# Banded attention and a SoLU layer on one core: one fixed instruction order replaced by another

## The chip, the cores and the metric

The kernel runs on one core of a Trainium2 chip. The core has a matmul engine (TensorE, "PE" in the profile, with its weight loads as "PEld"), three engines for elementwise work (VectorE "DVE", ScalarE "ACT", GpSimd "POOL"), and a queue engine ("SP") that issues most DMA transfers. Each engine runs its own list of instructions strictly in order and waits for the others by semaphores. The metric is the device time of one execution in microseconds; less is better.

## The reference

Two layers in a row. The first is attention over 4 batches, 8 heads, 768 tokens and head size 64, where a query sees the 96 keys up to its own position and the first 8 keys of the sequence ("global" keys), with a bias that falls with distance:

```python
scores = scale * np.matmul(q, k.transpose(0, 1, 3, 2))
is_global = pos[None, :] < int(n_global)
is_local = (rel >= 0) & (rel < int(n_local))
dist = np.where(is_global & ~is_local, float(n_local), np.abs(rel))
scores = np.where(is_global | is_local, scores - slopes * dist, -1e9)
a = np.exp(scores - max); a = a / (sum(a) + 1e-09)
x = (a @ v) as 3072 tokens x 512
```

The second is a feed-forward layer on the 3072 tokens, 512 to 1024 and back to 512:

```python
h = x @ w_in
solu = h * softmax(h)
ln = (solu - mean(solu)) / np.sqrt(var(solu) + 1e-06) * g_ln
out = ln @ w_out
```

## The kernel before

**Attention.** Heads go in pairs, so a batch `b` has four pairs `p`. For each pair, keys and queries are loaded (`x32`, 384 KB each), cast to 16 bit (`cast_k`, `cast_q`, to `x16`), transposed on TensorE (L728) and copied from PSUM ("evacuated") to `kT` and `qT`. Batch 3 takes a DMA transpose (L762) in place of TensorE and evacuation. Values are loaded in two pieces per pair (L486) and cast into `v16`. The scores of a pair are made in two groups (64-key blocks with a window of 160 queries each, L874), ACT takes their exponential into `eb` (L882). In batch 0 the distance bias is added by matmuls (L860); in batches 1 to 3 the exponentials are multiplied by a factor `fb` (L890) instead. The global keys have scores of their own (L927, exponential L940). For each half of a batch (384 tokens, "unit" 0 and 1) TensorE sums the exponentials (L954, L963), ACT takes the logarithm (L970), DVE splits it (L979), TensorE spreads it over the rows (L1009), and ACT turns it into reciprocals `rr` (L1018). The attention products (L1053, L1043) come in two parts with a tiny DVE copy, `tick` (L1063), between them, and DVE multiplies them by `rr` into `xT` (L1078).

**Feed-forward.** For each of 24 tiles of 128 tokens: eight matmuls with `w_in` (L1112, "the projection"), exponential `ef` on ACT (L1118), `u` on DVE (L1121), its squares on ACT (L1128) or DVE (L1132), a transpose of `u` (on TensorE, L1147, for tiles 0 to 4, by DMA, L1137, for 5 to 23), and eight matmuls with the prepared `w_out` (L1193). A few POOL or DVE steps and two ACT steps for each group of three tiles give `rstd` (L1167 to L1176), which scales the result on ACT (L1204) or DVE (L1207), and it is stored (L1211). The last tile is done in two halves. `w_out` is prepared by eight products with `g` (`gw`, L633 to L639) and eight centring steps (L650).

**Casts and copies.** The helper `copy` has one line per engine: L266 for ACT, L268 for DVE, L270 for POOL. What a row of those lines is shows in its tiles: `x<-x` is a cast of keys or queries, `kT<-acc` and `qT<-acc` an evacuation, `v<-v` a cast of values, `w_in_sb<-late` a cast of a `w_in` half, `bw<-bw` and `fb<-fb` the copies of the bias and of the factor.

**The order.** A `Plan` collects all steps with what they read, what they may run on and which buffers they take. Nothing is scheduled at run time: four tables of numbers at the top of the file settle it. `ORDER` is the sequence in which the steps are issued, and with that the order of each engine and of SP's transfers. `SLOTS` gives the buffer of each step that takes one. `ENGS` gives the engine of each step that may run on several (casts, evacuations, factor products `fac`, `gw`, squares, `stats`, the scaling of the result). `WARM` puts filler matmuls (L1220, on a tile of ones) into TensorE's list, as "place in the order : PSUM bank : count":

```python
for s in plan.order():
    for spot, count in s["warm"]:
        for _ in range(count):
            nc.tensor.matmul(out=acc[:, spot, :], lhsT=busy16[:, 0:P], rhs=busy16, start=True, stop=True)
    if s["fn"] is not None:
        s["fn"]()
```

Of the kernel before, what the change touches and what calls it, by code (L numbers as in the profile page):

```python
# [29 lines left out]
FACT = {1, 2, 3}  # L30
SPLIT = False
ORDER = """
# [30 lines left out]
"""  # L63
SLOTS = """
# [10 lines left out]
"""  # L75
ENGS = """
# [4 lines left out]
"""  # L81
WARM = """
25:0:16 30:2:4 37:3:2 48:5:3 59:3:2 117:7:4 156:6:5
"""


# [1172 lines left out]
```

## Time and profile before

| what | value |
|---|---|
| median of 3 runs | 154.12 us (154.05 to 154.29) |
| span of the profiled execution | 154.3 us |
| instructions | 4774 |
| granted TensorE clock | full in all slices of the page |
| DMA, mean over the span | 236 GB/s, 36.35 MB |
| SP's transfers, share of 16 DMA engines | 95.0% |

The profiled execution's own time is its span, 154.3 us, 0.2 above the runs' median. Rows of a timeline are: start, duration, engine, line, operation, tiles written and read, shapes, count, and in brackets the idle time before and what ended it. Rows of equal kind that follow each other are merged, so a duration with "x4" is that of four. Rows by stage give for each stretch its length, the busy time of PE, PEld, DVE, ACT and POOL with the number of instructions, the granted clock, the DMA share and GB/s.

### The profile page before, as it was taken

The numbers are of one execution on the slowest core, as the hardware profiler recorded it, in microseconds if no ns is written. First come the engines' busy times: TensorE is split into PE (matmuls) and PEld (weight loads), VectorE is DVE, ScalarE is ACT, GpSimd is POOL, SyncE is SP. The second block draws the span as 40 slices with busy tenths as digits, with TensorE's granted clock in tenths as the row PEclk, the third lists the DMA queues.
The fourth block names the chain that finished last, engine by engine and source line by source line (L and its number), as shares of the span: only waits on it lengthen the run. The fifth ranks groups of instructions, "written<-read, shape, count | busy, mean of one in ns | idle before, by whom it ended". The sixth has DMA issues, their size and how long they took to land.

```text
span 154.3 us, 4774 instructions
## 1 busy us (share of the span) xinstructions
PE 144.9 (94%) x1877; PEld 77.9 (50%) x1877; DVE 119.2 (77%) x241; ACT 123.4 (80%) x212; POOL 60.0 (39%) x145
## 2 busy tenths in 40 slices
PE   6988899999899999799999999999999999999991
PEld 2545556477554565644544644544445644444451
DVE  6749988899999994789799959399893885799200
ACT  3959999799999888499999887878885676884642
POOL 7574456565394626852813115454212000110000
PEclk9999999999999999999999999999999999999999
DMA  4999999999996997999999999998999954488743
GB/s 146 373 305 337 307 391 327 347 340 398 295 264 108 242 285 175 220 270 233 262 196 154 271 141 244 171 233 161 189 231 259 247 141 97 90 222 223 224 166 136
DMA packets 76429, 36.35 MB, mean 236 GB/s; under 512 B 65456, under 2 KB 71928, under 8 KB 76408
## 3 DMA queue, kind: packets, MB, share of 16 engines
q1 hardware_dynamic: 76120, 35.54, 95.0%
q10 hardware_dynamic: 288, 0.52, 0.9%
q8 instruction: 14, 0.23, 0.7%
q14 instruction: 7, 0.06, 0.1%
HBM read 23.15 MB, written 6.29 MB: 191 GB/s over the span
## 4 chain that ended last, share of the span: by engine, by line
PE 44%; DMA 19%; ACT 9%; DVE 8%; POOL 7%; SPq 5%; issue 5%; POOLq 0%; DVEq 0%; ACTq 0%
PE acc L1193 16%; PE acc L1112 15%; DMA v<-in_v_dram 6%; DMA x<-in_q_dram 5%; DMA qT<-x 4%; PE acc L1053 3%; DMA kT<-x 3%; SPq L486 3%; ACT eb L882 2%; POOL x L270 2%; PE acc L728 2%; PE acc L874 2%; DVE uu L1121 2%; ACT ef L1118 2%; ACT rr L1018 1%
## 5 line engine op out<-in xcount | busy, mean ns | idle before, releaser
L1112 PE MATMUL acc<-w_in_sb,xT 128*128 128x512 f16 x192 | 44.4, 379 | 0.0
L1193 PE MATMUL acc<-gw_out_sb,late 128*128 128x512 f16 (+1 forms) x200 | 44.3, 371 | 0.1
L1121 DVE SCALAR_TENSOR_TENSOR uu<-ef,acc 128x1024 f16<-128x1024 f16 x24 | 29.2, 1216 | 5.4 <-ACT ef L1118 5.0
L882 ACT ACTIVATE eb<-acc 128x896 f16<-128x896 f32 (+1 forms) x32 | 29.3, 960 | 1.8 <-PE acc L874 1.8
L1193 PEld LDWEIGHTS <-late 128*128 128x128 f16 x200 | 18.9, 98 | 21.1 <-issue 0.9
L1118 ACT ACTIVATE ef<-acc 128x1024 f16<-128x1024 f32 x24 | 24.8, 1035 | 5.8 <-PE acc L1112 5.4
L1112 PEld LDWEIGHTS <-xT 128*128 128x128 f16 x192 | 18.1, 98 | 21.3 <-issue 1.1
L270 POOL CAST x<-x 128x768 f16<-128x768 f32 x17 | 14.4, 851 | 22.8 <-DMA x<-in_q_dram 7.8
L1078 DVE TENSOR_TENSOR xT<-acc,rr 128x384 f16<-128x384 f32 x32 | 16.3, 549 | 3.6 <-ACT rr L1018 1.9
L1053 PE MATMUL acc<-eb,v 64*64 64x160 f16 (+4 forms) x448 | 16.5, 221 | 2.1 <-DVE xT L1078 1.6
L1053 PEld LDWEIGHTS <-v 64*64 64x64 f16 x448 | 12.9, 106 | 6.6 <-issue 4.3
L1128 ACT ACTIVATE sqa<-uu 128x1024 f16<-128x1024 f16 x15 | 16.1, 1071 | 0.0
L1018 ACT ACTIVATE rr<-acc 128x768 f32<-128x768 f32 x16 | 12.7, 809 | 4.1 <-DVE tick L1063 2.5
L890 DVE TENSOR_TENSOR eb<-eb,fb 128x896 f16<-128x896 f16 (+1 forms) x19 | 14.1, 769 | 0.8 <-ACT eb L882 0.8
L270 POOL CAST v<-v 128x704 f16<-128x704 f32 (+3 forms) x13 | 8.8, 685 | 10.0 <-DMA v<-in_v_dram 9.3
L1220 PE MATMUL acc<-busy 128*128 128x512 f16 x36 | 10.8, 443 | 1.5 <-DVE busy L545 1.5
L728 PE MATMUL acc<-ident,x 128*128 128x128 f16 x144 | 11.1, 220 | 0.8 <-ACT x L266 0.7
L874 PE MATMUL acc<-qT,kT 64*64 64x160 f16 (+2 forms) x384 | 11.4, 227 | 0.3 <-ACT qT L266 0.3
L1132 DVE SCALAR_TENSOR_TENSOR sqv<-uu 128x1024 f16<-128x1024 f16 x9 | 11.5, 1277 | 0.1
L890 POOL TENSOR_TENSOR eb<-eb,fb 128x960 f16<-128x960 f16 (+1 forms) x5 | 10.4, 2081 | 2.0 <-ACT eb L882 2.0
L1043 PE MATMUL acc<-eg,vgz 64*64 64x384 f16 x64 | 10.8, 324 | 0.0
L268 DVE CAST x<-x 128x768 f16<-128x768 f32 x8 | 5.6, 709 | 6.7 <-POOL slr L371 2.3
(120 smaller groups left out, 205.7 us busy)
## 6 DMA issues: line engine op xcount, KB each, us to landing
x<-in_q_dram SPq DMA_DIRECT2D x16, 384.0 KB, 6.0
x<-in_k_dram SPq DMA_DIRECT2D x16, 384.0 KB, 5.1
out_dram<-osb SPq DMA_DIRECT2D x12, 256.0 KB, 4.7
v<-in_v_dram SPq DMA_DIRECT2D x12, 192.0 KB, 4.0
out_dram<-x SPq DMA_DIRECT2D x9, 256.0 KB, 2.2
late<-in_moe_w_in_dram SPq DMA_DIRECT2D x4, 512.0 KB, 7.4
w_out<-in_moe_w_out_dram SPq DMA_DIRECT2D x4, 512.0 KB, 6.0
v<-in_v_dram SPq DMA_DIRECT2D x12, 160.0 KB, 4.0
```

The lines of the kernel that those rows point to most:

```text
L270: nc.gpsimd.tensor_copy(out=out, in_=in_)
L874: nc.tensor.matmul(out=sc[o : o + 64, par, col : col + n], lhsT=kk[r, BLK * c : BLK * c + BLK], rhs=qq[r, g0 : g0 + n], start=fresh, stop= ...
L882: ex["fn"] = (lambda ex=ex, qk=qk, gw=gw: nc.scalar.activation(out=eb[at(qk, "eb")][:, :, 0:gw], in_=big(qk)[:, :, 0:gw], func=AF.Exp, sca ...
L890: (nc.gpsimd if fx["at"] == "POOL" else nc.vector).tensor_tensor(out=e, in0=e, in1=fb[:, p, :, 0:gw], op=ALU.mult)
L1018: re["fn"] = lambda re=re, sp_=sp_, w=w: nc.scalar.activation(out=rr[at(re, "rr")][:, :, 0:w], in_=big(sp_)[:, :, 0:w], func=AF.Exp, scale ...
L1053: nc.tensor.matmul(out=o_[64 * h : 64 * h + 64, gl : gl + m], lhsT=vv[r, v_at(vi, h, c), pair, :], rhs=view(eb[at(e_own[b, gi, pair], "eb" ...
L1078: nc.vector.tensor_tensor(out=xT[at(xt_own[b], "xT")][:, p, q0:q1], in0=one(av, d)[:, 0:w], in1=rr[at(re, "rr")][:, d, 0:w], op=ALU.mult)
L1112: nc.tensor.matmul(out=ph()[:, ts(fh, 512)], lhsT=xT[at(xt_own[b], "xT")][:, j, ts(t % NA, P)], rhs=w_in_sb[:, j, ts(fh, 512)], start=(j = ...
L1118: ex["fn"] = lambda g1=g1, t=t, ph=ph: nc.scalar.activation(out=ef[at(g1, "ef")], in_=ph(), func=AF.Exp, accum_out=s0[:, t : t + 1])
L1121: u["fn"] = lambda u=u, g1=g1, t=t, ph=ph: nc.vector.scalar_tensor_tensor(out=uu[at(u, "uu")], in0=ef[at(g1, "ef")], scalar=USC, in1=ph(), ...
L1128: nc.scalar.activation(out=sqs_["ACT"], in_=uu[at(u, "uu")], func=AF.Square, scale=float(D_FF) ** 0.5, accum_out=s2[:, t : t + 1])
L1193: nc.tensor.matmul(out=one(g2)[:, 0:wd], lhsT=uT[at(el_o, "uT")][:, c, :], rhs=gw_out_sb[:, c, sl_], start=(c == 0), stop=(c == NFC - 1))
```

## The change

The four tables get new numbers; a row less in `ORDER` moves every later line up by one (L1220 is L1219 in the changed kernel). All steps, their shapes and their number stay. Every engine has another order, most of all before the first projection; from there on TensorE's list is that of before with neighbours exchanged here and there, until the last seventeen groups of matmuls of the feed-forward, which are ordered anew. 36 filler matmuls remain, at other places. These steps change engine: twenty-nine casts of keys, queries and values, three of `vends` (the values of a head's first or last 64 tokens), eight evacuations of keys and queries and one of `u`, nine factor products (six from DVE to POOL, three back), five `gw`, seven squares, six `stats`, eight scalings, five `w_in` halves and the queue of three stores. As sums: POOL has 8 factor products (5 before), 5 `gw` (2) and 16 casts of values (12); DVE has 16 factor products (19), 1 `gw` (5), 1 cast of values (4).

```diff
 ORDER = """
-126 86 12 11 271 2 13 17 16 10 15 66 14 18 0 20 73 36 3 75 7 1 4 88 68 69 89 22 53 55 56 90 8 70 38
+92 5 12 115 79 23 66 60 271 2 13 16 7 17 24 3 4 11 81 53 73 38 94 99 117 272 110 18 20 6 62 9 86 52 120
...
 ENGS = """
-1 0 0 1 1 1 1 1 2 0 2 1 0 0 2 0 1 0 1 0 0 0 1 2 2 2 1 1 2 0 0 1 1 1 1 0 1 2 2 0 2 1 2 1 0 1 0 0 1 1
+1 0 2 0 2 1 0 1 2 0 2 0 1 0 1 0 2 0 0 0 2 0 0 0 2 0 2 1 2 2 1 1 0 2 2 2 0 2 2 0 0 0 0 1 0 1 0 1 1 0 0 0 1
...
 WARM = """
-25:0:16 30:2:4 37:3:2 48:5:3 59:3:2 117:7:4 156:6:5
+5:1:3 7:0:16 14:1:5 33:1:2 39:0:4 49:5:2 105:1:4
 """
```

In `WARM`, all of the first five entries of the changed table (3, 16, 5, 2 and 4) come ahead of TensorE's first transpose; before, the first 16 did.

Three places, as the engines' lists show them. First DVE near its beginning; `pick`, `mlo` and `sgn` are small constants, `rf`, `junk`, `tick`, `gw_out_sb` and `gmask` belong to the constants of the global keys (`constants_far`). Before:

```order
L354 TENSOR_SCALAR sgn<-mlo 128x1
L268 CAST x_2_109<-x_1_101 128x768
L268 COPY bw<-bw 128x4x320
L268 COPY qT_122<-acc 128x768
L268 CAST x_1_108<-x_5_105 128x768
L268 COPY qT_121<-acc 128x768
L374 CAST rf<-ri 128x9
```

and of the change, from the same constant on:

```order
L353 TENSOR_SCALAR sgn<-mlo 128x1
L267 CAST x_0_107<-x_5_105 128x768
L373 CAST rf<-ri 128x9
L374 CAST gw_out_sb<-tgm 128x104
L375 SCALAR_TENSOR_TENSOR junk,gbias<-pick,slr 128x8
L377 SCALAR_TENSOR_TENSOR junk,tick<-pick,rf 128x8
L379 TENSOR_TENSOR tick<-rf,tick 128x1
L380 TENSOR_SCALAR gw_out_sb<-gw_out_sb,tick 128x104
L381 TENSOR_SCALAR gw_out_sb<-gw_out_sb 128x104
L383 TENSOR_SCALAR gw_out_sb<-gw_out_sb 128x104
L385 TENSOR_TENSOR gmask<-gw_out_sb 128x104
L267 COPY kT_120<-acc 128x768
```

The nine steps for the global keys moved ahead of the first evacuation; the `bw` copy follows behind two evacuations and two bias steps. Second, ACT ahead of the first projection's exponential (`ef`). Before, from the first logarithm:

```order
L970 ACTIVATE lns_142<-acc 128x384
L882 ACTIVATE eb_135<-acc 128x2x448
L882 ACTIVATE eb_138<-acc 128x960
L1018 ACTIVATE rr_146<-acc 128x768
L1018 ACTIVATE rr_147<-acc 128x768
L266 CAST w_in_sb<-late 128x512
L882 ACTIVATE eb_139<-acc 128x2x448
L266 CAST w_in_sb<-late 128x512
L970 ACTIVATE lns_143<-acc 128x384
L266 COPY kT_117<-acc 128x768
L1118 ACTIVATE ef_148,sums_92<-acc 128x1024
```

and of the change:

```order
L969 ACTIVATE lns_142<-acc 128x384
L881 ACTIVATE eb_133<-acc 128x2x448
L265 CAST w_in_sb<-late 128x512
L1017 ACTIVATE rr_147<-acc 128x768
L1017 ACTIVATE rr_146<-acc 128x768
L881 ACTIVATE eb_137<-acc 128x960
L265 CAST w_in_sb<-late 128x512
L265 COPY kT_116<-acc 128x768
L969 ACTIVATE lns_143<-acc 128x384
L881 ACTIVATE eb_134<-acc 128x2x448
L1117 ACTIVATE ef_149,sums_92<-acc 128x1024
```

Both `w_in` casts remain on ACT, the first ahead of the two `rr` exponentials, the second behind them and one more exponential. Third, DVE around batch 1's products into `xT_99`. Before:

```order
L1207 TENSOR_SCALAR osb_156<-acc,rstd 128x512
L1063 COPY tick<-acc 128x1
L979 SCALAR_TENSOR_TENSOR l_145<-lns_143,mlo 128x384
L1063 COPY tick<-acc 128x1
L1078 TENSOR_TENSOR xT_99<-acc,rr_146 128x384 x2
L268 CAST x_0_107<-x_2_102 128x768
L1078 TENSOR_TENSOR xT_99<-acc,rr_147 128x384 x2
L1063 COPY tick<-acc 128x1 x2
L268 COPY late<-acc 128x1024
```

and of the change:

```order
L1206 TENSOR_SCALAR osb_156<-acc,rstd 128x512
L1062 COPY tick<-acc 128x1
L978 SCALAR_TENSOR_TENSOR l_144<-lns_142,mlo 128x384
L1062 COPY tick<-acc 128x1
L1077 TENSOR_TENSOR xT_99<-acc,rr_147 128x384 x2
L267 COPY late<-acc 128x1024
L1077 TENSOR_TENSOR xT_99<-acc,rr_147 128x384 x2
L1062 COPY tick<-acc 128x1 x2
```

The cast between the two pairs of products, that of the last queries of batch 2, went to POOL; the evacuation of `u` of tile 3 (`late<-acc`) moved in between them. On SP's list, the query load of pair 2 of batch 3 (L479) went from place 69 to place 87, behind the DMA transposes of `u` of tiles 5, 9 and 10.

83 rows, old and new, of tables (ENGS, ORDER, SLOTS) are left out of this document.

## The prediction

> **What bounds the kernel now.** I read the page's first part and its groups first, then the table by stage, then the timeline and the waits of each engine where a stage has idle TensorE.
>
> ```profile
> PE 144.9 (94%) x1877; PEld 77.9 (50%) x1877; DVE 119.2 (77%) x241; ACT 123.4 (80%) x212; POOL 60.0 (39%) x145
> L1220 PE MATMUL acc<-busy 128*128 128x512 f16 x36 | 10.8, 443 | 1.5 <-DVE busy L545 1.5
> 24.00:28.00 4.00, 4.00 (x77) 2.35 (x67) 3.86 (x9) 3.62 (x6) 2.29 (x5) 1.00 1.10 319
> 40.00:50.00 10.00, 9.62 (x127) 5.15 (x120) 10.00 (x17) 10.00 (x17) 6.83 (x8) 1.00 0.95 207
> 60.00:64.00 4.00, 2.70 (x73) 2.09 (x75) 2.31 (x6) 1.34 (x3) 3.87 (x3) 1.00 0.62 143
> 80.00:90.00 10.00, 10.00 (x153) 5.19 (x153) 9.57 (x19) 8.62 (x18) 1.99 (x4) 1.00 1.21 203
> 116.00:118.00 2.00, 1.66 (x38) 0.93 (x40) 0.75 (x1) 1.35 (x2) 0.77 (x1) 1.00 1.18 281
> ```
>
> In a row by stage stand PE, PEld, DVE, ACT and POOL busy, the granted clock, the DMA share and GB/s. TensorE is busy 94% of the span, so the kernel is bound by its in-order stream almost everywhere; 10.8 us of that are the 36 filler matmuls (L1220), which compute nothing. The same 1877 matmuls, 36 fillers among them, are issued after the change. So only three things can move the end: when the first real stretch of matmuls begins, the holes in the stream, and the tail. At 40 to 50 DVE and ACT are full as well; at 60 to 64 TensorE alone has 1.3 us of holes, the largest after the start.
>
> **Step 1, the start.** These rows say when TensorE stops being a filler.
>
> ```profile
> 1.50 5.52 PE L1220 MATMUL acc<-busy 128*128 128x512 f16 x16 [1.50 <-DVE busy L545]
> 6.86 0.83 PE L728 MATMUL acc<-ident,x 128*128 128x128 f16 x12
> 25.92 1.24 PE L1220 MATMUL acc<-busy 128*128 128x512 f16 x5
> 27.00 1.89 PE L1112 MATMUL acc<-w_in_sb,xT 128*128 128x512 f16 x8
> ```
>
> Before, 16 fillers run from 1.50 to 6.86 (5.36 us, the first ones slow), then the first transposes; the last five take 25.92 to 27.00, 0.216 us each, and at 27.00 the first projection matmuls start. After the change 30 fillers (3+16+5+2+4) precede the first transpose: 1.50 + 5.36 + 14 x 0.216 = **9.88** instead of 6.86. From there the order hangs on DVE and ACT, whose rows are these:
>
> ```profile
> 5.71 1.10 DVE L268 COPY bw<-bw 128x1280 f16<-128x1280 f16 x1
> 7.73 0.96 DVE L268 COPY qT<-acc 128x768 f16<-128x768 f16 x1 [0.92 <-PE acc L728]
> 17.38 0.55 DVE L268 CAST x<-x 128x768 f16<-128x768 f32 x1
> 17.84 0.95 DVE L268 COPY qT<-acc 128x768 f16<-128x768 f16 x1
> 18.71 0.82 DVE L268 COPY fb<-fb 128x2560 f16<-128x2560 f16 x1
> 14.79 3.51 ACT L882 ACTIVATE eb<-acc 128x960 f16<-128x960 f32 x4 [0.33 <-PE acc L874]
> 18.15 1.07 ACT L940 ACTIVATE eg<-acc,gbias 128x384 f16<-128x384 f32 x2
> 20.88 0.49 ACT L970 ACTIVATE lns<-acc 128x384 f32<-128x384 f32 x1
> 22.91 1.69 ACT L1018 ACTIVATE rr<-acc 128x768 f32<-128x768 f32 x2
> 25.01 0.92 ACT L882 ACTIVATE eb<-acc 128x896 f16<-128x896 f32 x1
> 26.19 0.62 ACT L266 CAST w_in_sb<-late 128x512 f16<-128x512 f32 x1 [0.26 <-DMA late<-in_moe_w_in_dram]
> ```
>
> From start to start an evacuation costs DVE 0.87 us (17.84 to 18.71) and a cast 0.46 us (17.38 to 17.84). The nine `constants_far` steps now lie ahead of the evacuations, in DVE's wait for the first transpose, so they cost nothing as long as that wait lasts. An evacuation starts some 0.55 after its transposes (7.73, for the second six of the twelve that run from 6.86), so the first one at 10.4. Then stand, up to the first scores: two evacuations, two bias steps, the copy of `bw` (0.5 to 1.1) and one evacuation, 2 x 0.87 + 0.3 + 1.1 + 0.87 = 4.0: scores from 14.4, the first exponential at 15.0. Up to the last key and query that batch 0 needs stand three more evacuations, two casts and some 0.5 of waiting for the transpose of the late query load: 3 x 0.87 + 2 x 0.46 + 0.6 = 4.1, at 18.5. On ACT the six exponentials to `b0g0p3` are paced by this and by 0.9 each, and end at about 20.8; the first far exponential (0.6), one more exponential and the other far one bring the logarithm to 22.7, its end to 23.2. Then the split on DVE (0.64), the spread on TensorE (0.4 with its latency), two `rr` exponentials (1.69), one exponential (0.92) and the cast of a `w_in` half (0.62), which now stands behind them on ACT: 23.2 + 0.2 + 0.64 + 0.6 + 1.69 + 0.92 + 0.62 = 27.9. The four products into `xT` end at about the same time. The projection starts at **28.0, +1.0**.
>
> Bounds: before, the last `w_in` piece landed just ahead of 26.19; the changed list puts one 96 KB piece more in front of it, 0.3 us at 319 GB/s, so +0.3 is the lower end. With every evacuation and cast at its full 0.95 and 0.55 and a late `bw` copy the chain is 1.5 longer: +2.5 is the upper end. I take +1.0, from start-to-start times.
>
> **Step 2, the hole at 61 to 63.** The chain and three timelines belong together here.
>
> ```profile
> 53.34 7.72 DMA x<-in_q_dram
> 61.16 0.13 DVE x L268
> 62.05 1.02 DVE xT L1078 x2
> ```
>
> ```profile
> PE acc L1053 <- DVE xT L1078: 1.6, 3, 1.1
> 58.01 1.02 DVE L1078 TENSOR_TENSOR xT<-acc,rr 128x384 f16<-128x384 f32 x2
> 61.16 0.98 DVE L268 CAST x<-x 128x768 f16<-128x768 f32 x1 [2.12 <-DMA x<-in_q_dram]
> 62.05 1.01 DVE L1078 TENSOR_TENSOR xT<-acc,rr 128x384 f16<-128x384 f32 x2
> 62.65 0.26 PE L1053 MATMUL acc<-eb,v 64*64 64x160 f16 x2 [1.09 <-DVE xT L1078]
> 63.12 0.26 PE L1053 MATMUL acc<-eb,v 64*64 64x160 f16 x2 [0.21 <-DVE xT L1078]
> 60.12 1.60 POOL L270 CAST x<-x 128x768 f16<-128x768 f32 x2 [0.22 <-DMA x<-in_k_dram]
> 64.34 1.55 PE L728 MATMUL acc<-ident,x 128*128 128x128 f16 x24
> ```
>
> DVE stands idle from 59.0 to 61.16 in front of a cast of batch 2's last query load, which lands at 61.1. Behind it wait two ready products of batch 1, and behind those TensorE, for their PSUM banks. After the change this cast is on POOL, the products follow the evacuation of `u` of tile 3, and the attention product that waited takes other banks. The 1.09 and the other two waits of the row of 1.6 go: **-1.6**, which is also the most, and 0 if another wait takes their place. What is late next: the load itself still lands at 61.1 (53.34 + 7.72); POOL casts it in 0.8 (two in 1.60), and the transposes that need it stood at 64.34, so 2.4 are to spare, and about 1.7 if TensorE is 0.6 early. Between the start and here I keep the pace of before: DVE and ACT are full at 40 to 50, and in the new order DVE gives four of the eight `gw` products to ACT and POOL and takes evacuations for them.
>
> **Step 3, the last attention.**
>
> ```profile
> 117.12 0.26 PE L1053 MATMUL acc<-eb,v 64*64 64x160 f16 x2 [0.34 <-POOL v L270]
> ```
>
> TensorE waits 0.34 us for the cast of values of batch 3 that were loaded last. The casts of that batch go from POOL, POOL, ACT to ACT, DVE, ACT and the loads of the pair that was last now come third: **-0.3**, between 0 and -0.34. If TensorE gets here earlier, these loads have to be earlier as well; that is the rival below.
>
> **Step 4, the tail.**
>
> ```profile
> 150.18 1.86 SPq L1211 DMA_DIRECT2D out_dram<-x  x3
> 151.21 0.47 ACT L1204 ACTIVATE x<-acc,rstd 128x256 f32<-128x256 f32 x1 [0.40 <-PE acc L1193]
> ```
>
> The last half tile still ends the stream, is scaled by ACT and stored by SP. Ahead of it now stands a whole tile instead of its other half; its 256 KB store is issued about 0.6 before the last one. I take 0, with +0.2 as the other end.
>
> **Step 5, factor products on POOL.** [...]
>
> ```profile
> L890 POOL TENSOR_TENSOR eb<-eb,fb 128x960 f16<-128x960 f16 (+1 forms) x5 | 10.4, 2081 | 2.0 <-ACT eb L882 2.0
> 52.64 1.48 DVE L890 TENSOR_TENSOR eb<-eb,fb 128x896 f16<-128x896 f16 x1
> 52.60 1.04 POOL L508 TENSOR_TENSOR vgz<-vgn,pick 128x512 f16<-128x512 f32 x1
> 84.43 0.61 DVE L890 TENSOR_TENSOR eb<-eb,fb 128x896 f16<-128x896 f16 x1
> ```
>
> On DVE the same product took 0.61 alone and 1.48 where it began with a POOL operation: 0.87 more. Three products more on POOL spare DVE 3 x 0.61 and can stretch up to three DVE operations by 0.87: +0.8 at most where DVE is on the path, -1.8 at best where it is. I take 0, since TensorE's stream is full where most of them stand (as at 80 to 90). [...]
>
> **Sum.** 1.0 - 1.6 - 0.3 + 0 + 0 = -0.9 against the profiled span of 154.3: 153.4. The runs' median, 154.12, is 0.2 below that span, so the time to be measured is **153.2**.
>
> **Rivals.** First, *transfers decide*: DMA is at a share of 1.2 at 80 to 90 and 116 to 118, and the values of batch 3 land when they did. Then what is won by 63 is waited for at 117: the span is 154.3 again, 154.1 as measured. For it: nearly every stage from 64 on is full of DMA. Against: at 60 to 64 the share is only 0.62, because the list of SP was held, and the changed list takes one 384 KB query load out of that place. Second, *slower, the start runs through*: DVE's chain of evacuations begins 3 us later and is the longest of the start; from +1.9 on, a projection start after 28.9, it eats all that steps 2 and 3 win. At its upper end, +2.5, the sum is +0.6: 154.7; with the hole at 61 only moved, +2.5 - 0.3, 156.3. For it: DVE before had the idle 2.3 us at 9 to 11 in hand, and evacuated already at 7.7. Against: the changed order uses that idle time for `constants_far`. Third, *port*: the three products stretch DVE by 0.87 each where DVE is full, 2.6 in all, half of it on the path: 153.2 + 1.3 = 154.5.
>
> **How the numbers follow.** The forecast 0.5, transfers 0.2, the slow start 0.2, the port 0.1. Below 0.2% (153.8 to 154.4), about what a measurement of this kernel can tell from no change, lies the first rival; the other two are slower. So faster 0.5, same 0.2, slower 0.3. The range: below, +0.3 at the start with -1.6 and -0.34 gives 152.5, and 0.3 of step 5's gain 152.2; above, it takes in both slower rivals and 0.6 of a hole that moved: 155.3.
>
> **What would show it.** Step 1: the first row of L1112 at 28.0 (27.3 to 29.5), the first of L728 at 9.9. Step 2: no DVE cast behind a load at 59 to 61 and no hole over 0.5 at 60 to 64 on TensorE. Step 3: no wait of L1053 for a cast of v near 116. Step 4: 3.1 from the last scaling's start (151.21) to the end. Step 5: L890 on DVE between 0.6 and 1.5, no longer. The prediction is wrong if holes open elsewhere that the old trace can't show, above all on ACT, where a cast of batch 2's keys now stands ahead of an `rr` exponential, or if fillers end later than 9.9.

## The result and the profile after

The changed kernel takes **162.53 us** in the median (161.87 to 165.21, 4 runs), beside 154.20 for the kernel before (154.05 to 154.95, 4 runs), a difference of 8.3; the ratio measured side by side is 1.0497, 95% interval 1.0441 to 1.0553. It is slower by about 5%, where 153.2 with a range of 152.2 to 155.3 had been forecast. The profiled execution has a span of 160.7 and took 162.44. The run of 165.21 had a mean granted clock of 0.988 where the other three had 0.997 to 1.0, and the ratio is taken without it.

One number of the table ahead of the prediction needs a correction. There the profiled execution's own time was set equal to its span. In the later executions of the kernel before, the time lies 2.1 to 2.2 us above the span (155.51 against 153.4), in those of the changed kernel 1.7 (162.44 against 160.7). So the execution with the span of 154.3 will have taken about 156.4, and was itself some 2.3 longer than a median run, whose span would be about 152.0 (estimates from these differences). That is why the times differ by 8.3 and the two profiled spans by only 6.4. The tables below compare the profiled spans; how much of the slowdown is explained is judged by the times.

The page's first part and three of its groups, of the changed kernel:

```profile
PE 145.2 (90%) x1877; PEld 78.2 (49%) x1877; DVE 124.1 (77%) x242; ACT 120.9 (75%) x206; POOL 70.9 (44%) x150
L1192 PE MATMUL acc<-gw_out_sb,late 128*128 128x512 f16 (+1 forms) x200 | 44.3, 371 | 2.8 <-DVE osb L1206 1.7
L889 POOL TENSOR_TENSOR eb<-eb,fb 128x960 f16<-128x960 f16 (+1 forms) x8 | 16.0, 1996 | 11.3 <-ACT eb L881 6.8
L889 DVE TENSOR_TENSOR eb<-eb,fb 128x960 f16<-128x960 f16 (+1 forms) x16 | 14.4, 929 | 1.9 <-ACT eb L881 1.9
```

TensorE's busy time is nearly that of before (144.9); what grew is its holes. DVE gave three factor products away and is busy for 4.9 us longer. The rows by stage (columns as in the prediction) say where:

```profile
24.00:28.00 4.00, 2.82 (x96) 2.06 (x88) 3.15 (x9) 2.88 (x5) 1.88 (x4) 1.00 1.07 345
40.00:50.00 10.00, 8.28 (x113) 3.98 (x106) 8.12 (x15) 8.29 (x13) 5.95 (x8) 1.00 1.09 260
60.00:64.00 4.00, 4.00 (x89) 2.49 (x79) 3.03 (x8) 3.88 (x6) 4.00 (x6) 1.00 0.95 246
70.00:80.00 10.00, 8.34 (x72) 4.00 (x71) 9.49 (x14) 8.07 (x15) 7.36 (x6) 1.00 0.70 135
80.00:90.00 10.00, 8.98 (x130) 4.49 (x132) 9.76 (x15) 6.99 (x13) 4.56 (x7) 1.00 1.03 178
110.00:120.00 10.00, 8.36 (x100) 3.72 (x102) 8.49 (x14) 7.84 (x14) 3.11 (x4) 1.00 1.14 184
```

The hole at 60 to 64 is gone. Elsewhere TensorE is idle for 1.7 at 40 to 50, 1.7 at 70 to 80, 1.0 at 80 to 90 and 1.6 at 110 to 120; before, the stages at 70 and 80 had none, and at 70 to 80 DMA moved 232 GB/s where it now moves 135.

To compare executions of which each shifts the rest, the span is cut at the first matmul of six steps that stand in both orders: the first projection, the mean (the centring of `w_out`, L646), the last attention product of batch 1, the result product of tile 5, the first spread of batch 2, and the last result product. A piece ends at the first matmul of the step named. The lengths, from the traces; the third kernel is that of before with eight fillers fewer, a run further below whose span is close to that of a median run of before:

| kernel | to first projection | to mean | to end of batch 1 | to tile 5 | to spread of batch 2 | to last product | to end | span |
|---|---|---|---|---|---|---|---|---|
| before | 27.00 | 14.17 | 22.70 | 12.63 | 8.45 | 65.19 | 4.17 | 154.3 |
| before, eight fillers fewer | 27.89 | 14.18 | 20.90 | 12.64 | 8.45 | 64.58 | 4.17 | 152.8 |
| changed | 28.08 | 15.45 | 20.97 | 14.47 | 9.59 | 67.55 | 4.61 | 160.7 |
| changed less before | +1.08 | +1.28 | -1.73 | +1.84 | +1.14 | +2.36 | +0.44 | +6.4 |

The first and the third difference are the prediction's steps 1 and 2 (+1.0, -1.6). The rest had been put at nothing, but for the -0.3 of step 3. Beside the third kernel the changed one gains nothing in the piece to the end of batch 1 (20.97 against 20.90), and the last stages cost 3.0.

**Tile 5, +1.84.** Timelines of the changed kernel, first DVE, then POOL beside it, then TensorE's row behind them (start, duration, operation, idle time before):

```profile
71.15 1.72 DVE L889 TENSOR_TENSOR eb<-eb,fb 128x896 f16<-128x896 f16 x1 [0.44 <-ACT eb L881]
72.80 1.21 DVE L1120 SCALAR_TENSOR_TENSOR uu<-ef,acc 128x1024 f16<-128x1024 f16 x1
...
73.94 1.55 DVE L1166 TENSOR_TENSOR sq<-sums 128x6 f32<-128x6 f32 x1
75.52 0.68 DVE L1167 TENSOR_SCALAR sq<-sq 128x3 f32<-128x3 f32 x1
76.12 0.15 DVE L1168 TENSOR_TENSOR va<-sums,sq 128x3 f32<-128x3 f32 x1
76.30 0.62 DVE L1169 TENSOR_TENSOR va<-va,sq 128x3 f32<-128x3 f32 x1
76.84 1.41 DVE L889 TENSOR_TENSOR eb<-eb,fb 128x960 f16<-128x960 f16 x2
78.18 0.74 DVE L1206 TENSOR_SCALAR osb<-acc,rstd 128x512 f32<-128x512 f32 x1
```

```profile
70.39 2.00 POOL L889 TENSOR_TENSOR eb<-eb,fb 128x960 f16<-128x960 f16 x1 [2.36 <-ACT eb L881]
72.34 1.17 POOL L269 CAST v<-v 128x704 f16<-128x704 f32 x1
73.47 2.00 POOL L889 TENSOR_TENSOR eb<-eb,fb 128x960 f16<-128x960 f16 x1
75.41 1.49 POOL L269 CAST v<-v 128x704 f16<-128x704 f32 x2
```

```profile
78.97 0.38 PE L1192 MATMUL acc<-gw_out_sb,late 128*128 128x512 f16 x1 [1.66 <-DVE osb L1206]
```

The first operation of `stats g1` works on 6 columns and takes 1.55 us. It starts at 73.94 and ends at 75.49; POOL's factor product ends at 75.47. The factor product on DVE starts at 71.15 and ends at 72.87, 0.48 behind POOL's end at 72.39. Both DVE operations started while a POOL product ran, and neither ended before it was over. The four operations of `stats g1`, some 0.65 in all when nothing stands beside them (shown below), take 2.98. Behind them wait the scaling of tile 3 (78.18) and, for its PSUM bank, TensorE.

Beside five of the eight products on POOL stood a DVE operation that started during the product and ended 0.02 to 0.52 us behind its end: two factor products (at 71.15 and 117.24, the latter 2.33), the first operations of `stats g1` and of a later group (73.94 and 109.08), and a cast of keys or queries:

```profile
82.69 1.83 DVE L267 CAST x<-x 128x768 f16<-128x768 f32 x1
82.23 1.89 POOL L889 TENSOR_TENSOR eb<-eb,fb 128x896 f16<-128x896 f16 x1 [4.48 <-PE acc L926]
```

Set against the shortest of their own kind (0.61, 0.64, 0.16, 0.16 and 0.55), these five took 6.7 us longer in all; a sixth met the last 0.25 of a product and lost 0.11. These six operations read SBUF alone. DVE operations that read an input from PSUM (`u`, evacuations, scalings, centring) stood beside the same eight products and were at most 0.02 longer, as was a factor product that had begun 0.08 ahead of one (116.67). Before, beside two of POOL's five products no DVE operation took longer; beside the other three a cast lost 0.43 (61.16), a factor product 0.25 (73.65) and a cast 0.67 (100.41), 1.4 in all.

**The last stages, +2.36.** SP's list of the changed kernel:

```profile
73.24 6.05 SPq L1210 DMA_DIRECT2D out_dram<-osb  x2
80.67 1.24 SPq L1136 DMA_TRANSPOSE late<-uu  x1
82.01 2.09 SPq L761 DMA_TRANSPOSE kT<-x  x1
84.16 0.57 SPq L478 DMA_DIRECT2D x<-in_q_dram  x1
```

The second of the two stores in the first row is that of tile 3. It waits from 74.2 to 78.9 for the scaling that DVE is late with, then the transpose of `u` of tile 10 waits to 80.67; in the two 4 us slices from 76 on the page has 62 and 84 GB/s. Behind the late store stand five of batch 3's eight query and key loads, all its DMA transposes and all its values. Before, the same store stood nine places further back, with three of these five loads ahead of it; it is the second of the last row here, and SP did not wait for it:

```profile
76.32 1.43 SPq L762 DMA_TRANSPOSE kT<-x  x1
82.77 0.94 SPq L479 DMA_DIRECT2D x<-in_q_dram  x1
83.81 1.96 SPq L1211 DMA_DIRECT2D out_dram<-osb  x2
```

In the changed kernel SP issues from 82 on without a pause until 118, and TensorE's timeline shows the other end of it:

```profile
115.17 1.89 PE L1111 MATMUL acc<-w_in_sb,xT 128*128 128x512 f16 x8 [0.80 <-DVE osb L1206]
117.91 0.39 PE L1192 MATMUL acc<-gw_out_sb,late 128*128 128x512 f16 x1 [0.85 <-DMA late<-uu]
```

The `osb` scaling named there waits itself 0.84 for a store to free its buffer, the second for a DMA transpose that SP issued at 112.9.

### The profile page after: what moved, and what is told of

It reads as the page before. It is cut to its first block, busy times and chain, and to the rows that moved or that the text cites. A ratio compares the mean times of both kernels' runs of the same rounds, so it can differ in the third digit from the quotient of the medians.

```text
span 160.7 us, 4767 instructions
## 1 busy us (share of the span) xinstructions
PE 145.2 (90%) x1877; PEld 78.2 (49%) x1877; DVE 124.1 (77%) x242; ACT 120.9 (75%) x206; POOL 70.9 (44%) x150
## 5 line engine op out<-in xcount | busy, mean ns | idle before, releaser
L269 POOL CAST x<-x 128x768 f16<-128x768 f32 x16 | 15.4, 970 | 15.0 <-DMA x<-in_q_dram 5.5
L889 POOL TENSOR_TENSOR eb<-eb,fb 128x960 f16<-128x960 f16 (+1 forms) x8 | 16.0, 1996 | 11.3 <-ACT eb L881 6.8
L269 POOL CAST v<-v 128x704 f16<-128x704 f32 (+3 forms) x20 | 12.9, 667 | 14.8 <-DMA v<-in_v_dram 9.3
L1052 PE MATMUL acc<-eb,v 64*64 64x160 f16 (+3 forms) x448 | 15.7, 220 | 1.5 <-ACT lns L969 0.8
L889 DVE TENSOR_TENSOR eb<-eb,fb 128x960 f16<-128x960 f16 (+1 forms) x16 | 14.4, 929 | 1.9 <-ACT eb L881 1.9
L1127 ACT ACTIVATE sqa<-uu 128x1024 f16<-128x1024 f16 x14 | 14.8, 1060 | 0.3 <-DVE uu L1120 0.3
L873 PE MATMUL acc<-qT,kT 64*64 64x160 f16 (+2 forms) x384 | 12.0, 228 | 1.7 <-issue 1.5
L1131 DVE SCALAR_TENSOR_TENSOR sqv<-uu 128x1024 f16<-128x1024 f16 x10 | 12.8, 1281 | 0.1
L1219 PE MATMUL acc<-busy 128*128 128x512 f16 x36 | 10.2, 445 | 1.5 <-DVE busy L544 1.5
L727 PEld LDWEIGHTS <-x 128*128 128x128 f16 x144 | 8.6, 98 | 4.7 <-issue 1.0
```

The source lines that it names most:

```text
L269: nc.gpsimd.tensor_copy(out=out, in_=in_)
L727: nc.tensor.transpose(out=pt[:, ts(j, P)], in_=a[:, j, ts(pp, P)], identity=ident)
L889: (nc.gpsimd if fx["at"] == "POOL" else nc.vector).tensor_tensor(out=e, in0=e, in1=fb[:, p, :, 0:gw], op=ALU.mult)
L1052: nc.tensor.matmul(out=o_[64 * h : 64 * h + 64, gl : gl + m], lhsT=vv[r, v_at(vi, h, c), pair, :], rhs=view(eb[at(e_own[b, gi, pair], "eb" ...
L1127: nc.scalar.activation(out=sqs_["ACT"], in_=uu[at(u, "uu")], func=AF.Square, scale=float(D_FF) ** 0.5, accum_out=s2[:, t : t + 1])
```

## The experiments

Engines of steps are set by `ENGS`; the diffs below name the steps. Ratios are to the kernel before, measured beside each version. 'Port' in the expectations is a name for the stretch of DVE's operations measured above; no run shows a port.

**All `stats`, or all factor products, with the engines of before** (changed kernel else).

```diff
-stats g1 DVE, g2 DVE, g4 DVE, g6 DVE, g5 POOL, g7 POOL
+stats g1 POOL, g2 POOL, g4 POOL, g6 POOL, g5 DVE, g7 DVE
```

> The changed kernel with the engines of before for the six `stats` steps only (g1, g2, g4 and g6 back from DVE to POOL, g5 and g7 back to DVE). Theory 'port': in the changed kernel `stats g1` took DVE 2.98 us (its first operation 1.55 beside a POOL product, against 0.16 undisturbed) and TensorE waited 1.66 us at 77.3 behind the scaling that stands after it. With `stats` on POOL the scaling comes some 2 us sooner, the hole at 77 shrinks to under 0.6, that at 109 to 115 by some 0.5: 160.5 to 161.5. Rival 'order': DVE's list holds the scaling behind the factor products anyway, and what is freed is waited for in the next place: within 0.5 of 162.4.

Measured: 168.34 (ratio 1.086, 1.079 to 1.093), slower than the changed kernel, which neither theory allowed. The piece to tile 5 fell by 0.87 (13.60), about what was expected there; the last stages took 71.8 instead of 67.5. POOL and TensorE there:

```profile
105.54 0.84 POOL L270 CAST x<-x 128x768 f16<-128x768 f32 x1 [2.91 <-issue]
106.34 0.20 POOL L1167 TENSOR_TENSOR sq<-sums 128x6 f32<-128x6 f32 x1
```

```profile
108.54 1.00 PE L1112 MATMUL acc<-w_in_sb,xT 128*128 128x512 f16 x2 [4.84 <-ACT osb L1204]
```

`stats g4` now stands in POOL's list behind the cast of a load that comes late (it landed at 105.4); ACT's `rstd` and scaling wait for it, and TensorE for the bank.

```diff
-fac b1g1p3, b2g0p2, b2g1p0, b2g1p3, b3g0p0, b3g1p3 POOL; b1g0p2, b2g0p0, b3g1p0 DVE
+fac b1g1p3, b2g0p2, b2g1p0, b2g1p3, b3g0p0, b3g1p3 DVE; b1g0p2, b2g0p0, b3g1p0 POOL
```

> The changed kernel with the engines of before for the nine factor products (5 instead of 8 on POOL). Theory 'port': while a POOL factor product runs, DVE's operations in the changed kernel were 5.99 us longer in all than the same ones undisturbed (before: 0). Most of these products now go to DVE, 0.65 each, so DVE gains some 3 us between 70 and 118, and the holes at 77, 87 and 115 lose about half: 159.5 to 161. Rival 'order': the stretch lies beside other waits (rstd from ACT, landing stores): within 0.7 of 162.4.

Measured: 165.42 (1.066, 1.057 to 1.076). Tile 5 fell to 13.33 and the spread of batch 2 to 8.50, the length of before, but TensorE then stood 2.4 at 100 for a DMA transpose. Both theories failed on the time: the removal of the stretch shows at its place, and something behind it takes more than was won.

**All 84 engine choices exchanged**, once in the order of the changed kernel, once in that of before.

> The order, buffers and fillers of the changed kernel with all 84 engine choices of before. Theory 'port' (the choice of engines costs it): 156 to 159. Theory 'order' (the sequence itself costs it; engines chosen for another order fit it no better): 162 or more.

> The order, buffers and fillers of before with all 84 engine choices of the changed kernel. Theory 'port': most of the 8 us come with the engines: 158 to 161. Theory 'order': engines alone cost little: 154.5 to 157.

Measured: 193.75 (1.251, 1.246 to 1.256) and 177.55 (1.139, 1.131 to 1.147). The first is on the side of the rival ('order', 162 or more), the second outside both theories: the engines of one table under the order of the other are far worse than either kernel. Halves of the change can't be priced by exchanging whole tables, then; the next edits are small and local.

**Three factor products of batch 2 to DVE.**

```diff
-fac b2g0p2, b2g0p3, b2g1p3 POOL
+fac b2g0p2, b2g0p3, b2g1p3 DVE
```

> The changed kernel with three factor products of batch 2 (b2g0p2, b2g0p3, b2g1p3) moved from POOL to DVE, all else as changed. Theory 'port': beside these three, DVE was stretched by 1.10, 1.39 and 0.61 us at 71, 74 and 83; DVE takes 3 x 0.65 of work for it, of which only one product stands ahead of the scaling that TensorE waits for at 77.3. That wait falls from 1.66 to 0.6 or less, the one at 87.5 (1.0) to under 0.3, SP's store of tile 3 leaves some 1.5 us sooner: 160 to 161. Rival 'DVE is full there whoever runs them': the waits stay over 1.2 and 0.8, and the time within 0.5 of 162.4.

Measured: 164.00 (1.055, 1.049 to 1.062). The waits went as expected: tile 5 at 12.63 and the spread at 8.61, within 0.2 of before, 2.8 less than in the changed kernel. The time did not fall, for this row:

```profile
100.01 1.46 PE L1193 MATMUL acc<-gw_out_sb,late 128*128 128x512 f16 x3 [2.57 <-DMA late<-uu]
```

SP still issued the transpose of keys at 82.07 and batch 3's query load at 84.16, as in the changed kernel: its list held the transpose of `u` that TensorE, now earlier, ran into. Behind that hole the clock was granted at half for 3.4 us (the stage from 100 to 104 has 0.63).

**`stats g1` alone to POOL.**

```diff
-stats g1 DVE
+stats g1 POOL
```

> The changed kernel with `stats g1` alone moved from DVE to POOL. Theory 'port': DVE loses 2.98 us of operations that POOL's factor product had stretched, ahead of the scaling of tile 3; POOL runs them behind a cast of values at 73.5 and ends by about 75.5. The wait of 1.66 at 77.3 falls under 0.7, the store of tile 3 leaves SP some 1.5 sooner: 160 to 161.3; the wait of 4.8 of the run with all six `stats` changed (at 103) does not come, as it belongs to `stats g4`. Rival: POOL's list delays `rstd` by as much: within 0.5 of 162.4.

Measured: 163.26 (1.044, 1.036 to 1.052), not distinct from the changed kernel, nearer the rival's time, though by another way than POOL's list. Tile 5 at 13.60, half of what was hoped. DVE now meets POOL's second product with a factor product of its own:

```profile
77.12 2.31 DVE L890 TENSOR_TENSOR eb<-eb,fb 128x960 f16<-128x960 f16 x1 [0.49 <-ACT eb L882]
```

A product like the one just ahead of it, which took 0.65, takes 2.31: the stretch moved to the next operation. The 4.8 at 103 did not come.

**SP's list alone.** The store of tile 3 and the transpose of `u` of tile 10 go behind batch 3's loads:

```diff
-iss_store t3
-iss_uturn t10
 iss_turn_k b3p0
 iss_q b3p2
 iss_v b3 (one piece)
+iss_store t3
+iss_uturn t10
 iss_uturn t11
```

> The changed kernel with two rows of SP's list moved: the store of tile 3 and the DMA transpose of `u` of tile 10 go behind the DMA transpose of keys and the query and value loads of batch 3 that stood after them. In the changed kernel SP issued nothing from 74.2 to 78.9 (store of tile 3 waits for its scaling) and little to 80.7, the DMA engines moved 62 and 84 GB/s in those slices, and SP then issued without a pause up to 118, where TensorE waits 0.8 for a store to free an `osb` buffer and 0.85 for a DMA transpose. Theory 'SP blocked': the loads come some 5 us sooner, and both waits at 114 to 118 go, with the 0.67 at 122: 160.2 to 161.2. Rival 'DVE': the waits at 114 to 118 come from DVE's lateness, and stay: within 0.5 of 162.4.

Measured: 162.82 (160.62 to 163.5; 1.042, 1.031 to 1.054). The last stages took 64.48 instead of 67.55, and the waits at 114 to 122 are gone, as 'SP blocked' had it; the time is the rival's. SP:

```profile
76.23 0.98 SPq L1202 DMA_DIRECT2D out_dram<-osb  x1
77.31 1.27 SPq L753 DMA_TRANSPOSE kT<-x  x1
78.63 0.61 SPq L470 DMA_DIRECT2D x<-in_q_dram  x1
79.34 0.86 SPq L477 DMA_DIRECT2D v<-in_v_dram  x1
81.93 0.36 SPq L1202 DMA_DIRECT2D out_dram<-osb  x1
```

The loads leave behind the store of tile 1 at once. What was won doesn't show in the median. In the profiled execution TensorE ran at half clock for 3.4 us at 44; the fastest run, 160.62, is 1.25 under the fastest of the changed kernel. The holes that DVE causes at 78 and 88 stayed (14.47 and 10.15; the second piece is 0.56 longer).

**Both together.**

> The changed kernel with both: the three factor products of batch 2 on DVE, and the store of tile 3 and the DMA transpose of `u` of tile 10 moved down SP's list behind batch 3's loads. Alone, the first shortened TensorE's way from the second part of batch 1's attention to batch 2's spread by 2.8 us (21.2 against 24.1) but TensorE then stood 2.77 at 100 for a DMA transpose; alone, the second shortened the way from there to batch 3's spread by 3.1 (31.9 against 35.0) and left the waits on DVE. Theory 'two causes that add': both ways are short, 5.5 to 6 us less than the changed kernel in all, a span of 155 to 156 at full clock, and a time of 156 to 157.5. Rival 'one cause, seen twice' (what the one saves the other has saved already): a gain of 3 at most, 159.5 or more.

Measured: 158.44 (157.5 to 160.37; 1.0275, 1.021 to 1.034), the profiled execution at 157.5 with a span of 155.8: a time between the two forecasts. Tile 5 12.63, spread 9.15, last stages 64.71: in these pieces 5.1 us come back (2.3 and 2.8; alone, the edits gave 2.8 and 2.5 there), so the two add. In time the distance to the kernel before (154.83 beside it) falls from 8.3 to 3.6, and the ratio from 1.050 to 1.0275: these two causes are about half of the slowdown. Here `stats g1` shows what it takes with nothing beside it:

```profile
73.48 0.16 DVE L1159 TENSOR_TENSOR sq<-sums 128x6 f32<-128x6 f32 x1
73.68 0.17 DVE L1160 TENSOR_SCALAR sq<-sq 128x3 f32<-128x3 f32 x1
73.75 0.15 DVE L1161 TENSOR_TENSOR va<-sums,sq 128x3 f32<-128x3 f32 x1
73.94 0.16 DVE L1162 TENSOR_TENSOR va<-va,sq 128x3 f32<-128x3 f32 x1
```

Where the rest lies, the pieces tell (28.36, 14.40, 21.82, 12.63, 9.15, 64.71, 4.72). The start is 1.4 longer than in the profile of before. Against the third kernel of the table, whose own start is 0.9 late, 0.9 lies between the mean and the end of batch 1, 0.7 ahead of the spread of batch 2 and 0.55 at the end. What causes these three was not traced and stays open.

**Eight fillers fewer, in the same kernel.**

```diff
-5:1:3 7:0:16 14:1:5 33:1:2 39:0:4 49:5:2 105:1:4
+5:1:3 7:0:8 14:1:5 33:1:2 39:0:4 49:5:2 105:1:4
```

> The same with 8 of the 30 filler matmuls ahead of the first transposes left out (the second group has 8 instead of 16). Two questions. Start: theory 'the fillers hold the start back' (step 1): the first transposes come 1.7 to 1.9 us sooner, and the first projection by 0.5 to 1.0; rival 'casts and loads hold it' (the casts of pair 0 end at 10.6 and 11.3): under 0.3. The stall ahead of the mean: theory 'TensorE's own instructions are fetched late' (in every run so far the matmul numbered 606 or 607 of TensorE's list came 1.4 to 1.6 us behind the end of the fifth instruction transfer): the stall stays at number 606, which is now eight matmuls further in the program, inside the mean, and shrinks by about 1.5 as TensorE has that much more to do ahead of it; rival 'a semaphore of the mean': it stays ahead of the mean's first matmul with 0.7 to 2.4.

Measured: 158.08 (156.92 to 159.88; 1.019, 1.014 to 1.024). The first transposes came 2.1 sooner (7.58), the first projection did not (30.06, behind a stretch at half clock; 28.1 to 30.3 in the other runs with this start): so the fillers don't hold the start; that the casts and ACT's exponentials do is argued. The stall ahead of the mean went. The time is not distinct from that with the fillers.

**The cast of step 2 alone, in the kernel before; fewer fillers there; and both.**

```diff
-cast_q b2p3 DVE
+cast_q b2p3 POOL
```

> The kernel before with one cast moved, that of the queries of pair 3 of batch 2, from DVE to POOL. Step 2 of the prediction by itself: DVE no longer stands behind the load that lands at 61.1, the products of batch 1 run at 59, TensorE's 1.09 us of waiting at 61.5 and the two smaller waits go: 1.0 to 1.6 less than before, 152.6 to 153.2. Rival 'another wait takes its place' (POOL now stands before that load, with three casts behind it, and the transposes at 64.3 wait for them): 154.0 to 154.6.

Measured: 155.09 (0.998, 0.994 to 1.002), no difference, so a gain of 1.0 or more is excluded. The wait before the products of batch 1 is gone, the time isn't.

```diff
-25:0:16 30:2:4 37:3:2 48:5:3 59:3:2 117:7:4 156:6:5
+25:0:8 30:2:4 37:3:2 48:5:3 59:3:2 117:7:4 156:6:5
```

> The kernel before with 8 of its first 16 filler matmuls left out, all else as it is. Theory 'TensorE's instructions come late' (the matmul numbered 606 or 607 waits for the fifth instruction transfer, 0.51 us in the profile of before and 1.58 in that of the kernel with one cast moved, there with a half clock behind it): the number now falls eight matmuls further, inside the mean, and no gap over 0.3 is left ahead of the mean; 0.5 to 1.5 less than before, 153.0 to 153.9 beside 154.1 to 154.8. Rival 'the start': with fewer fillers TensorE's clock comes up later or falls again before the first projection, and that costs what the stall gives: 154 to 155.5.

Measured: 155.41 (1.001, 0.998 to 1.004), no difference, as the rival had it: the stall was gone, but the clock came up only at 10.3 us (5.4 before; a filler took 634 ns until then and 379 after), and the first projection 0.9 later. But this run, with every cast and order of before, has 20.90 from the mean to the end of batch 1, where the profile of before had 22.70:

```profile
59.34 1.89 DVE L268 CAST x<-x 128x768 f16<-128x768 f32 x1
61.16 1.01 DVE L1078 TENSOR_TENSOR xT<-acc,rr 128x384 f16<-128x384 f32 x2
58.82 2.00 POOL L890 TENSOR_TENSOR eb<-eb,fb 128x960 f16<-128x960 f16 x1 [0.94 <-ACT eb L882]
```

The load that DVE waited for to 61.16 had landed here before 59.34. The cast then took 1.89 instead of 0.55 beside a POOL product that ended at 60.82: the stretch of above, in the order of before. TensorE waited 0.19 behind it, not 1.09.

> The kernel before with both: 8 of the first 16 fillers left out and the cast of the queries of pair 3 of batch 2 on POOL. Theory: step 2 of the prediction holds from before's side too (the cast alone: ratio 0.998, its profiled run with a stall of 1.58 and a half clock ahead of the place), so the two add, 1 to 2 less than before and under the run with fewer fillers alone by 0.3 to 1.2: 152.4 to 153.4. Rival: what the cast gives is waited for later (transfers decide): the same as with fewer fillers alone, within 0.3.

Measured: 155.43 (1.004, 1.000 to 1.008). The rival holds: the cast adds nothing in time and shortens that piece by 0.2 (20.70).

No version that was tried is faster than the kernel before.

## Why the prediction was wrong

**Step 1 was right.** First transposes forecast at 9.9, first projection at 28.0; measured:

```profile
9.94 0.83 PE L727 MATMUL acc<-ident,x 128*128 128x128 f16 x12
28.08 0.60 PE L1111 MATMUL acc<-w_in_sb,xT 128*128 128x512 f16 x2
```

The six other runs with this start of the order and its 30 fillers lie between 28.36 and 30.32 (the last one behind a stretch at half clock), so 28.08 is an early one, and that +1.0 was met so closely is in part luck.

**Step 2 was right as a mechanism and wrong as a term.** The hole went (-1.73 in that piece). But it was a wait for a load that landed at 61.1 there, and before 59.34 in the run with fewer fillers in the kernel before, where TensorE's wait was 0.19 instead of 1.09 with no cast moved; and the cast alone gained nothing measurable. So the 1.6 most likely belonged to the execution that was profiled. The sum took 1.6 off that execution's span and then set the result beside the median of the times, from which nothing was to be had: without the term its own terms give +0.7, a little slower. No profile of a median run of before was taken, so this is argued from the run with fewer fillers.

**Where it broke** is the nothing that stood for all of 64 to 116. Two terms were missing.

- *Step 5, mis-sized.* "I take 0, since TensorE's stream is full where most of them stand": the stream was full because DVE was just in time. The price of 0.87 came from a POOL operation of 1.04, and there DVE's row ended 0.48 behind POOL's (54.12 and 53.64), as at 72.87 and 72.39 here: the price came near to what was left of the POOL operation (0.87 of 1.00 there, 1.11 of 1.24 and 1.39 of 1.53 here). A product of 1.9 to 2.3 on POOL cost the DVE operation beside it up to 1.7 (0.64 became 2.33 beside the last one, where the prediction allowed 1.5). The third rival ('port', 154.5) counted on this stretch; its three products at 0.87 were too little, because beside five of the eight on POOL a DVE operation now took longer, 6.7 in all, and because six `stats` had changed engine. I had listed those and cost them at nothing, and `stats g1` went from POOL into the path of a scaling that TensorE waits for. No run shows what holds the DVE operations, a port or anything else; the traces show that the five ended 0.02 to 0.52 behind POOL's end. The runs show the term by the edit that takes three products off POOL: -2.8 at that place.
- *SP's list, not walked.* I followed one query load past three transposes, and not what the store of tile 3 waits for when its scaling is late. It held SP for 4.7 us with most of batch 3's loads behind it. The first rival (*transfers decide*) was near this, but had the loads land "when they did", at 154.1. Shown by the run with only SP's list altered: 3.1 back in the last stages, 0.6 of it lost ahead of them.

Together they give back 5.1 in these pieces and about half of the slowdown in time, shown by the run with both. Of what is left, +1.1 to +1.4 at the start was forecast; some 2 in three other pieces stay open. The stall ahead of the mean (+1.28 here) comes in both orders (1.51 here, 1.39 in the run with the one cast), see below.

**Step 3**: no wait of TensorE for a cast of values near 116, as forecast; its 0.3 can't be told apart in the 2.4 by which the last stages grew. **Step 4**: from the last scaling to the end 3.5 instead of 3.1 (157.19 to 160.72), outside the +0.2 allowed; the cause is open.

## What to carry to other kernels

- A step moved between DVE and POOL is not priced by its own length. List what runs on the other engine at that moment: here a short DVE operation that read SBUF alone and started beside a POOL product ended 0.02 behind it (0.16 became 1.55), and all that stood behind it in DVE's list paid.
- In SP's list a store was a wait for the compute that feeds it (74.2 to 78.9). Walk the queue row by row with the new times; here a store that was 5 us late delayed every load behind it, and the bill came 30 us later.
- The hole behind a load in one profile (1.09 of TensorE) was 0.19 in another with the same casts and orders: what comes earlier there may simply be later elsewhere. And two gains that each vanished alone (164.00 and 162.82, beside 162.53) added when both were made (158.44). Before a gain is taken off a profiled execution, set that execution's own time beside the median: here it was some 2.3 longer.

## What was not expected of the hardware

**A wait of TensorE stood behind a transfer of the `instruction` queue.** The profile counts 14 transfers in a queue of that name, 0.23 MB or 16 KB each. In nine executions, of both orders, the matmul numbered 606 or 607 of TensorE's list starts 1.2 to 1.7 us behind the end of the fourth of these transfers that falls into the span (the expectations count one more; 1.6 in the changed kernel, 41.79 to 43.37, 1.5 in the profile of before), with 0.3 (before) to 2.1 of idle time ahead of it. The changed kernel's rows:

```profile
q8 instruction: 14, 0.23, 0.6%
```

```profile
43.37 0.23 PE L873 MATMUL acc<-qT,kT 64*64 64x160 f16 x1 [1.51 <-issue]
```

In that row the profile names no engine and no load that TensorE waited for ("issue"). In the 4.2 us ahead of the gap (37.40 to 41.63) TensorE started 128 matmuls, most of them small ones of attention; the fourth transfer began 3.3 us into them, at a DMA share of 1.10, and took 1.05. With eight fillers fewer ahead of it no such gap was left in the three kernels where that was tried (in two of them TensorE was idle for 0.26 and 0.31 in all at 40 to 50, the whole stage). That the transfer brings the matmuls that TensorE waits for, and that the data transfers delay it, is argued; no run shows it.

**The clock fell behind short gaps.** In the twelve profiled executions other than the two with all engines exchanged, it was granted at half for 3.41 us behind idle times of TensorE of 1.39, 1.69, 2.05, 2.14, 2.35, 2.57 and 4.84 us, once behind two of 1.0 and 0.7 close together, and not behind 1.51, 1.57, 1.66 and 1.67. So the length of the gap alone doesn't decide; what else does was not shown. In all of them the clock, once up, changed only after whole multiples of 3.413 us (11, 27 and 28 of them ahead of a fall, for instance; 44 or 150.19 us in the profile of before and 46 or 157.01 us in that of the changed kernel, both without a fall inside the span). A fall costs about 1.7 (half of 3.41, an estimate for a TensorE with no other wait), so a hole of 2 us may cost 2 or 3.7.
